# The order of the token products between the feature blocks of a mixer kernel

## The chip, the cores and the metric

The kernel runs on one core of a Trainium2 chip. The metric is the device time of one execution in microseconds (us). A core has five engines that run side by side, each working through its own instructions in their order: TensorE (PE, with its weight loads PEld), VectorE (DVE), ScalarE (ACT), GpSimd (POOL) and SyncE (SP). The last two mostly issue DMAs here.

## The reference

`x` has 8 batches of 4096 tokens with 192 features. A windowed weighted sum over the last seven tokens ("attention") comes first, with weights from a softmax; then a token mixer and a channel mixer, each with a ReLU between two matrix products:

```python
w = exp(weight_gen - max); w = w / (sum(w) + 1e-9)        # over 7 taps, 8 heads
x = einsum('bshk,bskhg->bshg', w, x_unfolded)             # each token with the six before it
h = maximum(x^T @ w_tok1, 0) @ w_tok2                     # over the tokens of a batch: 4096 -> 256 -> 4096
u = x + h^T
out = u + maximum(u @ w_ch1, 0) @ w_ch2                   # over the features: 192 -> 1536 -> 192
```

The four weight matrices come in as float64; the kernel converts them itself. Products are float32, or three float32r products of high and low parts.

## The kernel before, in words

Tokens are handled in 64 blocks (chunks) of 512, eight to a batch (`NCH = 8`, `NG = 64`). Four streams of work are laid into each other.

*Channel products.* Block `g` has six slots (`p` = 0 to 5, `NP = 6`). In each, `channel1(g, p)` multiplies u by 256 of the 1536 hidden columns (ten matmuls into the PSUM tile `ph`, line 496), ScalarE takes the ReLU (line 499) and VectorE the low part (line 500), and `channel2` multiplies the `h` of two slots before by the second weights (lines 514 and 516) into `acc`. It runs two slots behind, so slots 0 and 1 of block `g` still hold products of block `g - 1`; in slot 1 `store(g - 1)` adds `acc` to u (line 528) and writes the result out.

*Token products.* `token1(m)`, the first phase, multiplies chunk `m` of the attention's result by the first token weights and adds to `h1s` (lines 397, 398, 406 and 408; 415 in float32); after the eighth chunk of a batch the sum becomes `h1`. `token2_half(m, half)`, the second phase, multiplies `h1` by the second token weights of chunk `m`, in two halves (lines 449 and 450; 447 in float32), and VectorE adds the attention's result to give u (lines 456 and 458). So the second phase of a batch needs the first phase of all its chunks. Batches 0 and 1 do this in float32, the others in three float32r products; batch 2 makes the split weights and keeps them in DRAM.

*The pieces of u.* After the second half, `columns_of(m)` turns u from rows to columns: a transpose of 32x32 squares on VectorE (line 468), 24 copies on ScalarE in twelve items of two (line 476), then `split_u`: `a_hi` and the high part of `uc` on ScalarE (lines 424 and 425), `a_lo` and the low part of `uc` on VectorE (lines 426 and 429). `channel1(m, 0)` needs all of them.

*Attention.* VectorE makes chunk `m` in 13 operations (lines 200 and 208) and for every second chunk a softmax. A ring of nine buffers holds the results, so attention for chunk `m` waits until the second phase of chunk `m - 9` is done. `two_parts` then splits the chunk for the first phase (lines 222 and 225).

`ph`, the first phase's `th` and the second phase's `up` take turns in two PSUM buffers. `acc`, the token weights' tiles `w1` and `w2` and the tile `xh` have one buffer each.

The order is written by a planner in Python while the kernel is built. `at` holds its estimate of when TensorE, ScalarE and VectorE will be free, `on` adds an operation with its cost, and `pump(limit)` takes pieces from `chains` (the pieces of u, the attention, weight loads and splits) until VectorE is filled to `limit`. Column copies ("u", planned at 200 ns each) are taken only if they can start within 400 ns of the later of ScalarE and TensorE. What is issued decides the order on every engine; when it runs is settled on the chip by semaphores. At the end of each slot of block `g` there is room for one token product, and lines 820 to 830 choose it: the first phase of the next chunk, if it is ready and in slot 1 (`LAG - 1`) or less than eight chunks ahead of `g` (one more in the last block of a batch); else the next half of the second phase of chunk `g + 1`, if begun; else its first half, if `w2` and `h1` are in and the PSUM buffer is free by the plan. What is left after six slots is done at the end of the block.

Of the kernel before, what the change touches and what calls it, by code (L numbers as in the profile page):

```python
# [21 lines left out]
def mixer_kernel(ctx: ExitStack, tc: tile.TileContext, x, wg, wt1, wt2, wc1, wc2, out):  # L22
# [10 lines left out]
    NCH = S // N  # L33
# [5 lines left out]
    NG = B * NCH  # L39
    RING = NCH + 1  # L40
    F1, F2 = 2, 2
    LAG = 2
# [214 lines left out]
    w1t, w2t, rawt = {}, {}, {}  # L257
# [92 lines left out]
    def convert_channel(which, n, pool=None):  # L350
        out = []
        yield from convert(rawt.pop((which, n)), NF2 * D if which == "c2" else HF, out)
        yield "n", 0, lambda: raw_free()
        v, = out
        if which == "w1a":
            cs = slice(n * HF, (n + 1) * HF)
            yield from split(w1a_hi[:, cs], w1a_lo[:, cs], v)
        elif which == "c2":
            fs = slice(n * NF2, (n + 1) * NF2)
            yield from split(w2s[:, fs, 0:D], w2s[:, fs, D:2 * D], v.rearrange("p (f d) -> p f d", f=NF2))  # L360
        else:
            two = pool.tile([P, KA, CT, D], F32, tag="pr", name="prk", bufs=3)
            two = two.rearrange("p k t d -> p (k t d)").bitcast(F32R)
            hi, lo = two[:, 0:HF], two[:, HF:2 * HF]
            yield from split(hi, lo, v)
            for src, dst in ((hi, w1c_hi), (lo, w1c_lo)):
                for j in range(2):
                    for at in (0, DC):
                        yield "a", 730, lambda src=src, dst=dst, j=j, at=at: nc.scalar.copy(
                            dst[at:at + DC, j * HF:(j + 1) * HF], src[j * DC:(j + 1) * DC, :].bitcast(F32))  # L370

        def last():
            state["vals"] -= 1
            done.add((which, n))
        yield "n", 0, last

    h1s, h1t = {}, {}
# [10 lines left out]
    def token1(m):  # L388
        b, i = divmod(m, NCH)
        w = w1t.pop(m)  # L390
        th = ps_w.tile([P, 2, 512], F32, tag="w", name="th")
        if b >= F1:
            xh = xht.pop(m)
            for r in range(KR):
                for c in range(CT):
                    rs = slice(r * P, (r + 1) * P)
                    nc.tensor.matmul(th[:, r, 0:2 * D], w[:, c, 0, rs], xh[:, c, :], start=c == 0, stop=False)  # L397
                    nc.tensor.matmul(th[:, r, 0:D], w[:, c, 1, rs], xh[:, c, 0:D], start=False, stop=c == CT - 1)  # L398
        else:
            token1_float(th, w, m, 0, CT - 1)  # L400
        yield
        if i == 0:
            h1s[b] = late.tile([P, KR, D], F32, tag="h1s", name="h1s")
            nc.scalar.copy(h1s[b], th[:, :, 0:D])
        else:
            nc.vector.tensor_add(h1s[b], th[:, :, 0:D], h1s[b])
        if b >= F1:
            nc.vector.tensor_add(h1s[b], th[:, :, D:2 * D], h1s[b])
        if i == NCH - 1:
            make_h1(b, h1s.pop(b))  # L410
# [124 lines left out]
    at = {"pe": 0.0, "act": 0.0, "dve": 0.0}  # L535
# [5 lines left out]
    SLACK0 = 1000  # L541
    SLACK_M = 400
    LATE = 300
    FIRST = 0
    C1, C2 = 2290, 2264
    TOP, LOW = 1040, 1135
    h_at, w_at, h1_at = {}, deque([0.0, 0.0]), {0: 0.0}
    free = {"acc": 0.0, "u": 0.0}
    ready = deque()

    def on(engine, cost, *after):
        at[engine] = max(at[engine], *after, 0.0) + cost
        return at[engine] + HOP

    class Chain:
# [4 lines left out]
        def next(self):  # L560
            self.item = next(self.items, None)
# [19 lines left out]
    def add_chain(items, wait=None):  # L581

        chains.append(Chain(items, max(at["pe"], at["dve"]) + LOAD if wait is None else wait))

    def pump(limit):

        scalar = not state["rush"] and any(c.item is not None and c.item[0] == "u" for c in chains)
        while True:
            best = None
            for c in chains[1:] + chains[:1]:  # L590
                if c.blocked() or c.item is None:
                    continue
                kind = c.item[0]
                if kind == "u":

                    start = max(at["act"], c.wait)
                    end = max(at["pe"], w_at[0]) + C1 + LATE
                    if state["late"] or start <= max(at["act"], at["pe"]) + 400 and start + c.item[1] <= end:
                        best = c
                        break  # L600
                    continue
                if kind in "as" and c.wait > max(at["act"], at["pe"]):
                    continue
                if kind == "s":
                    if scalar == 0:
                        scalar = 1
                        best = c
                        break
                    continue
                if kind in "an":  # L610
                    best = c
                    break
                start = max(at["dve"], c.wait)
                if best is None or start + 100 < max(at["dve"], best.wait):
                    best = c
            chains[1:] = [c for c in chains[1:] if c.item is not None or c.blocked()]
            if best is None:
                return
            if best.item[0] == "v" and max(at["dve"], best.wait) + best.item[1] > limit:
                return  # L620
            best.issue()
# [54 lines left out]
    with tc.tile_pool(name="pro", bufs=1) as pro:  # L676
# [9 lines left out]
        def start(items):  # L686

            items = iter(items)
            for _ in range(4):
                next(items)[2]()  # L690
            return items
# [48 lines left out]
        last = start(convert_channel("w1a", 1))  # L740
# [21 lines left out]
    def do_token1():  # L762
        m, t = ready.popleft()
        it = token1(m)
        next(it)
        end = on("pe", 2264 if m >= F1 * NCH else 2600, t, w_at.popleft())
        state["token1"] = m
        pump(end + SLACK_M)
        next(it, None)
        w_at.append(on("dve", 1000 if m >= F1 * NCH else 500, end))  # L770
        if m % NCH == NCH - 1:
            h1_at[m // NCH] = on("act", 420, w_at[-1])
            if m >= F2 * NCH:
                h1_at[m // NCH] = on("dve", 480, h1_at[m // NCH])
        if m + 1 < NG:
            add_chain(load_w1(m + 1))
# [17 lines left out]
    def token1_ready():  # L794
        return ready and ready[0][0] in w1t and ready[0][1] <= at["pe"] + 100

    for g in range(NG + 1):
        parts = None if g + 1 < NG else iter(())
        state["rush"] = g == 0
        for p in range(NP if g < NG else LAG):  # L800
            if g == 0:
                need(lambda: (2 * p + 2) * P <= HF or ("w1a", 1) in done)
            if g == 0 and p >= LAG:
                need(lambda: ("c2", 2 * (p - LAG) // NF2) in done)
            if g < NG:
                channel1(g, p)
                end = on("pe", C1, w_at.popleft(), free["u"] if p == 0 else 0.0)
                end = on("act", TOP, end)
                h_at[g, p] = on("dve", LOW, end)
                w_at.append(h_at[g, p])  # L810
            n = g * NP + p - LAG
            if n >= 0:
                prev = divmod(n, NP)
                channel2(*prev)
                on("pe", C2, h_at.pop(prev), free["acc"] if prev[1] == 0 else 0.0)
            if p == LAG - 1 and g > 0:
                store(g - 1)
                free["acc"] = on("dve", 2000, at["pe"] + HOP) - 570
            pump(next_lo() + (SLACK if g > NCH else SLACK0))
            if token1_ready() and (p == LAG - 1 or ready[0][0] < g + NCH + ((g + 1) % NCH == 0)):  # L820
                do_token1()
            elif parts is not None:
                next(parts, None)
            elif p >= FIRST and g + 1 in w2t and (g + 1) // NCH in h1t \
                    and max(w_at[0], h1_at[(g + 1) // NCH]) <= at["pe"]:
                parts = do_token2(g + 1)
                next(parts)
            else:
                continue
            pump(next_lo() + SLACK)  # L830
        if parts is None:
            need(lambda: g + 1 in w2t)
            while (g + 1) // NCH not in h1t:
                need(token1_ready)
                do_token1()
            parts = do_token2(g + 1)
        for _ in parts:
            pass
        if g + 1 < NG:
            need(lambda: g + 1 in ut)  # L840
# [29 lines left out]
```

## Time and profile before

| | |
|---|---|
| three runs, median | 2344.61 us (2344.28 to 2345.2) |
| the profiled execution, its own time | 2343.91 us |
| its span in the profile | 2342.1 us |
| busy: TensorE, VectorE, ScalarE | 2196.7, 1842.1, 1085.0 us |
| matmuls | 12256 |
| mean granted TensorE clock | 0.978 |

The times of the page and of the time lines count from the span's start; a line such as L496 is that line of the kernel. A row of a group gives its line, engine, operation, output and inputs, shape, count, busy time and the mean in ns, then the idle time before it. A row of waits names who waited for whom, the sum in us, how often, and the longest. A matmul's busy time overlaps with the next one's, so the time between starts tells more than the durations. Block 0 begins after the prologue, at 129.7 us; the last block has a tail in which only `store` is left.

### The profile page before, as it was taken

Reading aid. Unit: us, or ns where it says so; the run is one execution under the profiler, and the core shown is the slowest. Engines: PE = TensorE matmul, PEld = TensorE weight load, DVE = VectorE, ACT = ScalarE, POOL = GpSimd, SP = SyncE. Lnnn points to the kernel's source line nnn. Section 1 sums busy time; section 2 is a strip of 40 time slices with the busy share of each in tenths; the row PEclk is TensorE's granted clock in tenths of the full one; section 3 lists DMA queues with packets and bytes.
Section 4 is the critical chain, followed back from the end, with each engine's and each line's share of the span. In section 5 each row is a group of like instructions: output and inputs, shape, how many; then the busy total and the mean of one; then the engine's idle time right before and its main releaser. Section 6 shows DMA issues by size and latency. Waiting matters only on the chain.

```text
span 2342.1 us, 30675 instructions
## 1 busy us (share of the span) xinstructions
PE 2196.7 (94%) x12256; PEld 1962.0 (84%) x12256; DVE 1842.1 (79%) x2231; ACT 1085.0 (46%) x2265; POOL 58.4 (2%) x104
## 2 busy tenths in 40 slices
PE   7869989999998999999999999999999999999998
PEld 5558878888887888888888888888888888899997
DVE  8889887878876888879887888869887798844443
ACT  4675443544534355345434434444443454344443
POOL 0000000000000000000000000000000000000000
PEclk9989999999999999999999999999999999999999
DMA  7733131223241333313332232332233132211110
GB/s 282 233 133 140 63 106 70 100 97 114 92 156 62 108 113 135 120 64 124 123 107 99 105 122 80 116 112 104 101 107 120 63 124 103 73 55 46 46 42 21
DMA packets 52127, 244.69 MB, mean 104 GB/s; under 512 B 6008, under 2 KB 15736, under 8 KB 38672
## 3 DMA queue, kind: packets, MB, share of 16 engines
q1 hardware_dynamic: 43360, 196.58, 24.3%
q0 software_dynamic: 8624, 46.14, 4.9%
q8 instruction: 97, 1.59, 0.3%
q14 instruction: 46, 0.38, 0.0%
HBM read 192.36 MB, written 50.33 MB: 104 GB/s over the span
## 4 chain that ended last, share of the span: by engine, by line
PE 38%; ACT 19%; DVE 14%; issue 11%; DMA 1%; POOL 0%; POOLq 0%; ACTq 0%; SPq 0%; DVEq 0%
PE ph L496 17%; ACT a_f L476 9%; PE acc L514 9%; ACT c_f L476 4%; PE acc L516 4%; ACT h L499 4%; DVE h L500 3%; DVE xa L208 3%; PE th L397 3%; DVE pr L200 3%; PE up L449 2%; DVE uc L429 1%; PE th L398 1%; DVE a_lo L426 1%; DMA w<-s 1%
## 5 line engine op out<-in xcount | busy, mean ns | idle before, releaser
L514 PE MATMUL acc<-w2s,h 128*128 128x384 f32 x3072 | 902.1, 358 | 0.0
L499 ACT ACTIVATE h<-ph 128x1024 fp32r<-128x1024 f32 x384 | 392.8, 1023 | 1004.4 <-PE ph L496 980.3
L516 PE MATMUL acc<-w2s,h 128*128 128x192 f32 x3072 | 773.5, 252 | 0.0
L500 DVE SCALAR_TENSOR_TENSOR h<-ph,h 128x1024 fp32r<-128x1024 f32 x384 | 468.3, 1220 | 294.3 <-ACT h L499 292.7
L516 PEld LDWEIGHTS acc<-w2s,h 128*128 128x128 f32 x3072 | 591.3, 192 | 16.0
L514 PEld LDWEIGHTS acc<-w2s,h 128*128 128x128 f32 x3072 | 583.3, 190 | 16.0
L496 PE MATMUL ph<-a_hi,w1a_hi 128*128 128x512 f32 x768 | 321.6, 419 | 58.9 <-ACT a_hi L424 33.9
L496 PE MATMUL ph<-uc,w1c_hi 128*128 128x512 f32 x768 | 311.7, 406 | 44.2 <-DVE uc L429 44.2
L200 DVE TENSOR_TENSOR pr<-xt,wn 128x768 f32<-128x768 f32 x336 | 318.2, 952 | 4.1
L208 DVE TENSOR_TENSOR xa<-xa,pr 128x768 f32<-128x768 f32 x336 | 319.7, 952 | 1.0
L496 PE MATMUL ph<-a_lo,w1a_hi 128*128 128x512 f32 x768 | 306.8, 399 | 6.0 <-DVE a_lo L426 6.0
L476 ACT COPY a_f<-t 32x128 f32<-32x128 f32 x1024 | 302.6, 295 | 16.6 <-DVE t L468 5.5
L496 PE MATMUL ph<-a_hi,w1a_lo 128*128 128x512 f32 x768 | 305.6, 398 | 0.0
L496 PE MATMUL ph<-uc,w1c_lo 128*128 128x512 f32 x768 | 305.2, 397 | 0.0
L496 PEld LDWEIGHTS ph<-uc,w1c_hi 128*128 128x128 f32 x768 | 146.6, 191 | 97.6 <-DVE uc L429 49.4
L496 PEld LDWEIGHTS ph<-a_hi,w1a_hi 128*128 128x128 f32 x768 | 146.5, 191 | 87.4 <-ACT a_hi L424 37.3
L496 PEld LDWEIGHTS ph<-a_lo,w1a_hi 128*128 128x128 f32 x768 | 146.6, 191 | 45.8 <-DVE a_lo L426 14.4
L496 PEld LDWEIGHTS ph<-uc,w1c_lo 128*128 128x128 f32 x768 | 147.4, 192 | 30.1
L496 PEld LDWEIGHTS ph<-a_hi,w1a_lo 128*128 128x128 f32 x768 | 148.0, 193 | 16.0
L476 ACT COPY c_f<-t 32x128 f32<-32x128 f32 x512 | 152.0, 297 | 7.4
L528 DVE TENSOR_TENSOR ur<-acc,ur 128x384 f32<-128x384 f32 x256 | 136.2, 553 | 8.3 <-PE acc L516 3.9
L449 PE MATMUL up<-h,w 128*128 128x384 f32 x384 | 116.4, 359 | 0.0
(70 smaller groups left out, 1914.8 us busy)
## 6 DMA issues: line engine op xcount, KB each, us to landing
w<-s SPq DMA_DIRECT2D x80, 1024.0 KB
xt<-in_x_dram SPq DMA_DIRECT2D x56, 960.0 KB
out_dram<-ur POOLq DMA_DIRECT2D x63, 384.0 KB, 4.9
raw<-in_moe_w_tok_dram SPq DMA_DIRECT2D x16, 1024.0 KB
s<-w POOLq DMA_DIRECT2D x16, 1024.0 KB, 4.1
val<-s SPq DMA_DIRECT2D x24, 512.0 KB
wg<-in_weight_gen_dram SPq DMA_DIRECT2D x64, 112.0 KB
s<-val SPq DMA_DIRECT2D x8, 512.0 KB
```

Source lines behind the costliest of these rows:

```text
L200: nc.vector.tensor_mul(dst.rearrange("p t (h g) -> p (t h) g", h=H).rearrange("p (o n) g -> p o n g", o=1), x_k, w)
L208: nc.vector.tensor_add(box["acc"], box["acc"], box.pop(k))
L397: nc.tensor.matmul(th[:, r, 0:2 * D], w[:, c, 0, rs], xh[:, c, :], start=c == 0, stop=False)
L398: nc.tensor.matmul(th[:, r, 0:D], w[:, c, 1, rs], xh[:, c, 0:D], start=False, stop=c == CT - 1)
L449: nc.tensor.matmul(up[:, j, 0:2 * D], w[:, k, 0, cs], h1[:, k, :], start=k == 0, stop=False)
L476: nc.scalar.copy(dst[to:to + Q, :].rearrange("p (c n j) -> p c n j", c=CT, n=NQ)[:, :, n, :], box["t"][n * Q:(n + 1) * Q, :, d, :])
L496: nc.tensor.matmul(ph[:, j, :], w[:, fs], u, start=n == 0, stop=n == len(steps) - 1)
L499: nc.scalar.activation(h[:, :, 0, :], ph, AF.Relu)
L500: nc.vector.scalar_tensor_tensor(h[:, :, 1, :], ph, 0.0, h[:, :, 0, :].bitcast(F32), op0=ALU.max, op1=ALU.subtract)
L514: nc.tensor.matmul(ps[:, 0:2 * D], h[:, j, 0, cs], w2s[:, f, :], start=f == 0, stop=False, **kw)
L516: nc.tensor.matmul(ps[:, 0:D], h[:, j, 1, cs], w2s[:, f, 0:D], start=False, stop=f == NF - 1, **kw)
L528: nc.vector.tensor_add(u[:, t, :], a[:, :, l * D:(l + 1) * D], u[:, t, :])
```

## The change: both halves of the second phase in consecutive slots, then the first phase

Only the choice of the token product at the end of a slot changes. `halves` marks that the second half is still to come. The first phase goes first only in the last block of a batch as long as the batch that follows has no `h1`. Otherwise a begun second phase is finished in the next slot; the first half of chunk `g + 1` is taken as soon as it is possible, with 300 ns of tolerance in the test; and then the first phase of chunks up to `g + 8`, in any slot. The constant `FIRST` was 0 and goes.

```diff
+        halves = []
...
-            if token1_ready() and (p == LAG - 1 or ready[0][0] < g + NCH + ((g + 1) % NCH == 0)):
+            last = (g + 1) % NCH == 0 and (g + 1) // NCH not in h1t and g + 1 < NG
+            if token1_ready() and last:
                 do_token1()
-            elif parts is not None:
+            elif parts is not None and len(halves) > 0:
+                halves.pop()
                 next(parts, None)
-            elif p >= FIRST and g + 1 in w2t and (g + 1) // NCH in h1t \
-                    and max(w_at[0], h1_at[(g + 1) // NCH]) <= at["pe"]:
+            elif parts is None and g + 1 in w2t and (g + 1) // NCH in h1t \
+                    and max(w_at[0], h1_at[(g + 1) // NCH]) <= at["pe"] + 300:
                 parts = do_token2(g + 1)
                 next(parts)
+                halves.append(1)
+            elif token1_ready() and ready[0][0] <= g + NCH:
+                do_token1()
             else:
                 continue
             pump(next_lo() + SLACK)
```

More of the change, by code (lines that the diff above doesn't have):

```diff
@@ L543, in mixer_kernel @@
     LATE = 300
-    FIRST = 0
     C1, C2 = 2290, 2264
```

## The prediction

> **What bounds the kernel now.** I read the totals first, then TensorE's waits, then busy time by stretches, then the time lines of VectorE and ScalarE around the waits.
>
> ```profile
> PE 2196.7 (94%) x12256; PEld 1962.0 (84%) x12256; DVE 1842.1 (79%) x2231; ACT 1085.0 (46%) x2265; POOL 58.4 (2%) x104
> ```
> ```profile
> PE ph L496 <- DVE uc L429: 44.2, 54, 2.3
> PE ph L496 <- ACT a_hi L424: 33.9, 12, 9.7
> PE ph L496 <- DVE h L500: 24.6, 28, 7.0
> ...
> PE ph L496 <- DVE a_lo L426: 6.0, 3, 3.2
> ```
>
> TensorE bounds it, and nearly all its idle time lies ahead of ph, the first channel product. For 84.1 us (44.2 + 33.9 + 6.0) it waits for the split pieces of u (a_hi, a_lo, uc) at the start of a block, and for 24.6 us until VectorE has emptied the PSUM buffer that the next ph takes. What this costs is seen block by block: in the next rows the columns are stretch, length, then busy us of PE, PEld, DVE, ACT and POOL, the granted clock and the DMA. The bounds are starts of blocks: 1 to 7, 8 to 14, 15 to 22, 31 to 38, then the pair 31 and 32, the six 33 to 38, then single blocks 28, 29, 33 and 57, and three short stretches behind waits.
>
> ```profile
> 167.40:425.80 258.40, 241.71 (x1335) 217.06 (x1334) 220.47 (x264) 130.19 (x252) 9.49 (x15) 0.97 0.28 99
> 425.80:674.40 248.60, 234.57 (x1319) 212.23 (x1317) 204.22 (x249) 113.78 (x244) 9.12 (x16) 0.98 0.27 100
> 674.40:968.30 293.90, 270.50 (x1505) 242.18 (x1506) 238.08 (x297) 130.56 (x279) 9.13 (x16) 0.96 0.32 115
> 1241.30:1514.40 273.10, 262.04 (x1507) 237.13 (x1506) 229.02 (x289) 122.48 (x271) 5.36 (x9) 0.99 0.30 106
> 1241.30:1313.20 71.90, 67.45 (x378) 60.70 (x377) 50.51 (x65) 30.78 (x70) 1.08 (x2) 0.95 0.28 101
> 1313.20:1514.40 201.20, 194.59 (x1131) 176.43 (x1130) 178.50 (x225) 91.70 (x202) 4.29 (x7) 1.00 0.31 108
> 1141.00:1174.50 33.50, 32.49 (x191) 29.46 (x190) 30.40 (x40) 15.46 (x35) 1.59 (x2) 1.00 0.31 104
> 1174.50:1207.90 33.40, 32.40 (x190) 29.34 (x189) 27.07 (x34) 14.87 (x34) 0.54 (x1) 1.00 0.32 112
> 1313.20:1347.30 34.10, 32.51 (x190) 29.43 (x189) 32.05 (x40) 14.76 (x33) 0.54 (x1) 1.00 0.30 109
> 2122.10:2151.60 29.50, 29.50 (x174) 27.11 (x173) 13.82 (x18) 14.08 (x32) 0.54 (x1) 1.00 0.14 50
> 1279.90:1285.40 5.50, 4.81 (x11) 3.29 (x12) 2.25 (x3) 0.49 (x1) 0.00 (x0) 0.50 0.00 0
> 498.80:502.40 3.60, 3.60 (x18) 3.60 (x17) 2.98 (x4) 1.02 (x1) 0.00 (x0) 0.62 0.53 156
> 533.00:536.60 3.60, 3.16 (x18) 2.89 (x19) 3.29 (x5) 1.03 (x1) 0.00 (x0) 1.00 0.00 0
> ```
>
> Block 57 has no first-phase product and no attention, and TensorE never stops: 29.5 us. One first-phase product takes 2.27 us (1152.78 to 1155.05 below), so a block without waits takes 31.8. Block 29 takes 33.4: 1.6 lost. The pair 31 and 32, where a batch ends, takes 71.9 against 63.6: 8.3 lost. The time line of TensorE in block 28 shows where, and behind it stand three waits of other blocks.
>
> ```profile
> 1146.09 0.36 PE L449 MATMUL up<-h,w 128*128 128x384 f32 x1
> ...
> 1148.13 0.50 PE L496 MATMUL ph<-a_hi,w1a_hi 128*128 128x512 f32 x1 [0.74 <-DVE h L500]
> ...
> 1152.78 0.36 PE L397 MATMUL th<-xh,w 128*128 128x384 f32 x1
> ...
> 1155.05 0.41 PE L496 MATMUL ph<-a_hi,w1a_hi 128*128 128x512 f32 x1
> ...
> 1160.77 0.42 PE L496 MATMUL ph<-a_hi,w1a_hi 128*128 128x512 f32 x1
> ...
> 1175.57 0.51 PE L496 MATMUL ph<-uc,w1c_hi 128*128 128x512 f32 x1 [0.27 <-DVE uc L429]
> ```
> ```profile
> 496.77 0.47 PE L496 MATMUL ph<-uc,w1c_hi 128*128 128x512 f32 x1 [2.29 <-DVE uc L429]
> ...
> 533.44 0.47 PE L496 MATMUL ph<-uc,w1c_hi 128*128 128x512 f32 x1 [2.29 <-DVE uc L429]
> ...
> 1279.92 0.80 PE L496 MATMUL ph<-a_hi,w1a_hi 128*128 128x512 f32 x1 [3.15 <-ACT a_hi L424]
> ```
>
> Slot 0 holds a half of the second phase (1146.09), slot 1 the first phase, slot 2 the other half, which ends at 1160.77. At batch ends two first-phase products come ahead, so the halves sit in slots 2 and 3 and the wait grows to 3.15 us. A long wait also costs clock: behind it the clock was 0.50 for 5.5 us.
>
> **The change part by part.** No operation is added or removed. *The second half moves from slot 2 to slot 1*, past one slot and one first-phase product. From 1155.05 to 1160.77 is one slot with a half, 5.72 us; less that half's own 1.13 (it has half the matmuls of a first-phase product) that is 4.6 for the slot, and 2.27 for the product gives 6.9 us earlier. What follows it is the chain that makes u's pieces: the transpose, 24 column copies, the casts, the two subtractions. In block 28:
>
> ```profile
> 1162.16 0.98 DVE L468 STREAM_TRANSPOSE t<-ur 128x768 f32<-128x768 f32 x1
> ...
> 1174.83 0.69 DVE L429 TENSOR_TENSOR uc<-c_f,uc 64x512 fp32r<-64x512 f32 x1
> ```
> ```profile
> 1164.25 4.90 ACT L476 COPY a_f<-t 32x128 f32<-32x128 f32 x16
> ...
> 1169.69 1.01 ACT L499 ACTIVATE h<-ph 128x1024 fp32r<-128x1024 f32 x1
> 1170.72 1.84 ACT L476 COPY c_f<-t 32x128 f32<-32x128 f32 x6
> ```
>
> It ran from 1160.77 to 1175.52, 14.8 us, and uc is wanted 0.7 us after the block's start (1175.57 less the 0.27 waited). It is late by tenths; 6.9 us earlier it has over 6 to spare. Then the 0.74 wait for h in slot 0 is next: VectorE empties ph late there because u was late and because products of the attention stand ahead of it. Attention for a chunk is let in by the second half nine chunks before, so it too starts a slot and a product earlier, and fewer of its operations reach the next slot 0. I keep 0.4 us per block (between none, as in block 57, and 0.9, the 0.74 with its delay): half of the blocks have a softmax in the same slots. The copies have a cost of their own: a copy takes 0.31 us (4.90 for 16), the planner counts 0.2, so 24 of them may stand 2.5 us longer than planned ahead of the ReLU of slot 3, as 18 did ahead of the one at 1169.69. I count nothing: the buffer that this ReLU and VectorE empty is wanted again in slot 5, two slots (9.1 us) after its own ph began, of which ph takes 2.3, ReLU and VectorE's pass 2.3. Past 4.5 us of lateness TensorE would stop there by the excess. *The first phase moves from slot 1 to slot 2.* Its cast of the next xh and its two adds go with it. The cast waits on ScalarE for the product's end, now behind copies; its chunk is wanted a block later, over 25 us of cover. *DMAs:* w2's reload now stands ahead of w1's in SP's queue; each has one buffer and is wanted again over 20 us later (w2 after four slots and a product, w1 after a block). The chain of waits has one such load at the batch's end:
>
> ```profile
> 1248.91 4.78 DMA w<-s
> ```
>
> It takes 4.8 us, so both stay hidden, and the back-to-back first-phase products that waited for it disappear. POOL's stores follow the same operations in the same order. *At batch ends* the one product that is needed comes first, then the halves in slots 1 and 2, one slot earlier than now. I keep 1.6 us for the next block's start, as in block 29 (whose halves ended in slot 2), 0.4, and 0.5 for the new hidden cost there: the sums and ReLU of the first phase now have one slot of 4.55 us (between 0 and 1.3). That leaves 2.5 of 8.3. *The 0.3 us of tolerance* in the test for the first half lets it into slot 0 more often; cost nothing, since the slot would hold it anyhow.
>
> **Sum.** Against 31.8 a block. Blocks 33 to 38: 201.2 - 190.8 = 10.4, left 2.4, saved 8.0; pair: 8.3 - 2.5 = 5.8. Four groups of eight like this (23 to 54): 4 x 13.8 = 55. Blocks 15 to 22: 293.9 - 254.6 = 39; split of the second weights rides on VectorE there, I leave 12: 27. Blocks 8 to 14: 248.6 - 222.7 = 26; waits of 2.29 and the clock behind them go, float32 products stay, leaving 7: 19. Blocks 1 to 7: 36; VectorE is busy 220.5 of what would be 223, so it soon bounds: 22 left, 14 saved. Together 115. The profiled execution took 2343.9 (median 2344.6): **2229 us**. Bounds: the 0.4 between 0 and 0.9 for some 44 blocks, 15 to 22 left with 5 to 25, the rest by 8: 2200 to 2262.
>
> **The rivals.**
>
> *A: as forecast, 69%.* For it: block 57 has the new order and its pieces are done 4.4 us ahead of the block's end at 2151.6.
>
> ```profile
> 2146.52 0.69 DVE L429 TENSOR_TENSOR uc<-c_f,uc 64x512 fp32r<-64x512 f32 x1
> ```
>
> *B: VectorE takes half of it back, 20%.* Block 33 is against A: in block 32 the halves sat in slots 0 and 1, with attention, yet block 33 took 34.1.
>
> ```profile
> 1294.05 2.20 DVE L528 TENSOR_TENSOR ur<-acc,ur 128x384 f32<-128x384 f32 x4
> ...
> 1299.74 0.97 DVE L468 STREAM_TRANSPOSE t<-ur 128x768 f32<-128x768 f32 x1
> ```
> ```profile
> 1302.14 1.02 ACT L499 ACTIVATE h<-ph 128x1024 fp32r<-128x1024 f32 x1 [2.87 <-PE ph L496]
> 1303.06 4.89 ACT L476 COPY a_f<-t 32x128 f32<-32x128 f32 x16
> ```
>
> The store and an attention add stood ahead of the transpose, and the copies stood behind the ReLU of slot 3, though the transpose ended at 1300.7. Block 32 had no first-phase product in slot 2; the issue of copies behind such a product, which the new order has, is what lets them in before. Where VectorE still lags, 0.8 us stays in steady blocks, 5 in the pairs, and half in 1 to 22: 4 x (5.6 + 3.3) + 28 gives 64 saved, 2280.
>
> *C: a pile-up in slot 1, slower, 6%.* There VectorE now has h, the four stores (2.20) and two adds (with their wait 1.4, from 1160.77 to 1162.16), and ph and the accumulators of slot 2 wait for them. The stores of block 32 ended at 1296.25, 1.1 us before they were wanted (from their start on, a half of 1.13 and a ph of 2.3 were still to come). Beyond a lag of 1.1 us TensorE stops. A softmax adds 3.3 us of VectorE in every second block (30.40 in block 28 against 27.07 in 29).
>
> ```profile
> L200 DVE TENSOR_TENSOR pr<-xt,wn 128x768 f32<-128x768 f32 x336 | 318.2, 952 | 4.1
> ```
> ```profile
> 1151.79 1.23 DVE L500 SCALAR_TENSOR_TENSOR h<-ph,h 128x1024 fp32r<-128x1024 f32 x1 [0.60 <-ACT h L499]
> ```
>
> If the softmax and one such product (0.95) stood ahead of h there, 3.15 us would be lost, the very wait of block 32, and behind it 5.5 us at half clock (2.75): 5.9 in 27 blocks is 159, and 2388. It decides from 115 / 27 = 4.3 us lost in each on. Against it: VectorE stood idle for 0.60 before h in slot 1 of block 28, softmax and all. [...]
>
> *D: the halves stay where they are, 5%,* because w2 or the buffer isn't ready in the planner's slot 0: 2344. Against it: blocks from 8 on begin their first half there already.
>
> **How the numbers follow.** About 0.2% (4.7 us) can be told from no change. A and B are faster, and a little of D: 0.89; D and edges: 0.04; C: 0.07. 2195 to 2300 leaves out C, D and thin edges of A and B, under 2 in 10.
>
> **What would show it.** Right: TensorE's waits for uc and a_hi fall from 78 to under 25 us; steady blocks near 32.2, the pair near 66, clock above 0.95 there; copies start in slot 2. Wrong: waits for h (24.6 now) grow past 40 (B), waits in slot 2 for h or the accumulators (C), or first halves still ahead of a first-phase product (D).

## The result, and the profile after

The changed kernel takes 2270.76 us (median of four runs, 2268.67 to 2271.11) against 2344.45 us for the kernel before: a ratio of 0.9685, 95% interval 0.9669 to 0.9702, some 74 us faster. The forecast was 2229 us with a range of 2195 to 2300, so the direction and the range held, but only two thirds of the 115 us came. One execution of all that follow, of the kernel with the copies at 300 ns, ran at a mean granted clock of 0.654 (0.991 in the others) and took 2949.67 us; the ratio given there is of the other three.

The waits of TensorE in the changed kernel (who waited for whom, sum in us, times, longest):

```profile
PE ph L496 <- DVE h L500: 49.7, 37, 6.6
...
PE ph L496 <- DVE h1s L408: 9.9, 6, 3.0
PE ph L496 <- ACT a_hi L424: 9.7, 1, 9.7
PE ph L496 <- DVE uc L429: 3.3, 7, 1.1
```

Before, the three pieces of u cost 84.1 us of waiting; now 13.0, of which one wait of 9.7 is block 0's and was there before. But the wait for h, the emptying of the PSUM buffer, has doubled from 24.6 to 49.7 us, and there is a new one, for `h1s`.

Busy time by stretches of the changed kernel, in the columns of the prediction: blocks 1 to 7, 8 to 14, 15 to 22, the pair 31 and 32, the six 33 to 38, and the single blocks 28 (with a softmax) and 29 (without).

```profile
169.00:414.50 245.50, 235.37 (x1333) 214.40 (x1333) 223.41 (x267) 130.03 (x252) 9.51 (x15) 0.99 0.31 108
414.50:651.30 236.80, 229.65 (x1318) 209.46 (x1317) 204.13 (x251) 114.77 (x245) 8.59 (x15) 0.99 0.30 107
651.30:923.30 272.00, 260.29 (x1505) 236.84 (x1505) 236.78 (x296) 129.41 (x277) 9.66 (x17) 0.99 0.34 124
1190.00:1257.20 67.20, 65.18 (x378) 58.99 (x377) 55.81 (x71) 31.23 (x69) 1.08 (x2) 1.00 0.30 107
1257.20:1457.30 200.10, 194.42 (x1130) 177.89 (x1129) 173.76 (x219) 91.36 (x201) 4.29 (x7) 0.99 0.31 109
1091.00:1124.40 33.40, 32.15 (x189) 29.47 (x189) 30.30 (x40) 15.52 (x34) 1.59 (x2) 1.00 0.32 105
1124.40:1156.60 32.20, 32.09 (x189) 29.41 (x189) 27.09 (x34) 14.94 (x33) 0.54 (x1) 1.00 0.33 116
```

The pair fell from 71.9 to 67.2 us and its clock rose from 0.95 to 1.00: the 3.15 us wait and the slow products behind it are gone. The six blocks hardly moved, from 201.2 to 200.1. A block without softmax now takes 32.2, close to the 31.8 without waits; one with softmax still takes 33.4. What it loses is lost in one place, in slot 0, behind the first half (1095.5 to 1096.7):

```profile
1097.93 0.50 PE L496 MATMUL ph<-a_hi,w1a_hi 128*128 128x512 f32 x1 [1.25 <-DVE h L500]
```

The cause lies a block earlier. ScalarE and then VectorE of the changed kernel from slot 2 on (block 28; the same shape stands in block 27):

```profile
1107.19 4.90 ACT L476 COPY a_f<-t 32x128 f32<-32x128 f32 x16
1112.12 2.46 ACT L476 COPY c_f<-t 32x128 f32<-32x128 f32 x8
1114.61 0.62 ACT L424 CAST a_hi<-a_f 128x512 fp32r<-128x512 f32 x1
...
1115.65 0.83 ACT L222 CAST xh<-xa 128x768 fp32r<-128x768 f32 x1
1116.39 1.02 ACT L499 ACTIVATE h<-ph 128x1024 fp32r<-128x1024 f32 x1
```
```profile
1115.26 0.69 DVE L426 TENSOR_TENSOR a_lo<-a_f,a_hi 128x512 fp32r<-128x512 f32 x1 [1.57 <-ACT a_hi L424]
1116.51 0.96 DVE L225 TENSOR_TENSOR xh<-xa,xh 128x768 fp32r<-128x768 f32 x1 [0.56 <-ACT xh L222]
...
1118.20 1.23 DVE L500 SCALAR_TENSOR_TENSOR h<-ph,h 128x1024 fp32r<-128x1024 f32 x1
```

All 24 copies, both casts of u and the cast of xh stand in one piece ahead of slot 3's ReLU. The planner's price decides this: besides the test on a copy's start, it takes a copy only if, at that price, it ends no later than 0.3 us after the end of the next channel product (lines 596 and 597 of the changed kernel). At 24 times 200 ns all of them pass; they take 7.4 us. VectorE, whose next operations need their results, stands idle for 1.57 and 0.56 us, then works without a gap, and is still behind when slot 0 of the next block comes. In slot 0 of block 28, behind the same row of copies in block 27, h starts at 1096.66, two microseconds after the end of its ReLU (1093.34 and 1.03 long).

```profile
1093.34 1.03 ACT L499 ACTIVATE h<-ph 128x1024 fp32r<-128x1024 f32 x1 [3.53 <-PE ph L496]
...
1096.66 1.22 DVE L500 SCALAR_TENSOR_TENSOR h<-ph,h 128x1024 fp32r<-128x1024 f32 x1
```

Over the whole kernel these two waits of VectorE come to 98 us:

```profile
DVE a_lo L426 <- ACT a_hi L424: 66.1, 48, 3.3
...
DVE xh L225 <- ACT xh L222: 31.9, 39, 2.0
```

The other new wait is in slot 4 of the first block of a batch (block 32). The first chunk's first-phase product is not added but copied out of PSUM, by ScalarE (line 404), and that copy stands behind 14 column copies:

```profile
1241.67 4.30 ACT L476 COPY a_f<-t 32x128 f32<-32x128 f32 x14 [3.10 <-DVE t L468]
...
1246.72 0.47 ACT L404 COPY h1s<-th 128x384 f32<-128x384 f32 x1
...
1247.22 0.56 DVE L408 TENSOR_TENSOR h1s<-th,h1s 128x384 f32<-128x384 f32 x1 [3.88 <-ACT h1s L404]
```
```profile
1247.83 0.50 PE L496 MATMUL ph<-a_hi,w1a_hi 128*128 128x512 f32 x1 [1.08 <-DVE h1s L408]
```

The theory from here on, L: what is left is VectorE's lag, made in slot 3 by copies that the planner takes for shorter than they are. Rival F: VectorE is simply full in the blocks with a softmax (30.3 us busy). Rival V: the planner's prices of VectorE's own operations are too low.

### The profile page after: what moved, and what is told of

The parts are those of the page before. It is cut to its first block, busy times and chain, and to the rows that moved or that the text cites. A ratio compares the mean times of both kernels' runs of the same rounds, so it can differ in the third digit from the quotient of the medians.

```text
span 2269.1 us, 30604 instructions
## 1 busy us (share of the span) xinstructions
PE 2161.0 (95%) x12256; PEld 1948.0 (86%) x12256; DVE 1843.1 (81%) x2231; ACT 1085.4 (48%) x2265; POOL 58.4 (3%) x104
## 3 DMA queue, kind: packets, MB, share of 16 engines
q8 instruction: 97, 1.59, 0.3%
## 4 chain that ended last, share of the span: by engine, by line
DVE 31%; issue 31%; ACT 19%; PE 17%; DMA 1%; POOL 1%; POOLq 0%; SPq 0%; ACTq 0%; DVEq 0%
PE ph L496 10%; ACT a_f L476 8%; DVE h L500 8%; DVE xa L208 6%; DVE pr L200 5%; ACT c_f L476 4%; PE acc L514 3%; ACT h L499 3%; PE acc L516 2%; DVE prk L240 1%; DVE ur L528 1%; DVE uc L429 1%; ACT xh L222 1%; DVE xh L225 1%; PE up L449 1%
## 5 line engine op out<-in xcount | busy, mean ns | idle before, releaser
L496 PE MATMUL ph<-a_hi,w1a_hi 128*128 128x512 f32 x768 | 319.3, 416 | 71.1 <-DVE h L500 49.7
L476 ACT COPY a_f<-t 32x128 f32<-32x128 f32 x1024 | 302.6, 296 | 43.4 <-DVE t L468 32.1
L496 PE MATMUL ph<-uc,w1c_hi 128*128 128x512 f32 x768 | 303.0, 395 | 3.3 <-DVE uc L429 3.3
L496 PEld LDWEIGHTS ph<-uc,w1c_lo 128*128 128x128 f32 x768 | 145.5, 189 | 31.9
```

Of the source, the lines that this page charges most:

```text
L476: nc.scalar.copy(dst[to:to + Q, :].rearrange("p (c n j) -> p c n j", c=CT, n=NQ)[:, :, n, :], box["t"][n * Q:(n + 1) * Q, :, d, :])
L496: nc.tensor.matmul(ph[:, j, :], w[:, fs], u, start=n == 0, stop=n == len(steps) - 1)
```

## The experiments

**Which part of the change gave what.** One kernel has the new choice only in the last block of each batch, another in all other blocks:

```diff
+            new = (g + 1) % NCH == 0        # the other kernel: != 0
+            if not new and <the old choice> ...
+            elif new and <the new choice> ...
```

> The new choice only in the last block of each batch, the old one in all others. If the parts add up: the pairs around a batch's end give 4 x 4.7 (71.9 to 67.2 us), the pair 15 and 16 some 9 and 7 and 8 none, so about 28 of the 74 us: 2316. If the clock gate made most of it, the pairs alone give 40 and more: under 2305.

Measured: 2300.87 us, ratio 0.9817 (0.9802 to 0.9831): 43 us of the 74, so the last blocks alone give more than the 28 expected, and the time is that of the second case. The pair 31 and 32 and the six behind it in that kernel:

```profile
1218.30:1284.10 65.80, 64.53 (x378) 58.73 (x377) 57.25 (x73) 31.18 (x70) 1.08 (x2) 1.00 0.31 110
1284.10:1484.70 200.60, 194.61 (x1130) 176.35 (x1129) 172.37 (x217) 90.95 (x202) 4.29 (x7) 1.00 0.31 108
```

The pair is better than in the full change (65.8 against 67.2), the six about the same (200.6, 200.1). That the clock made most of the 43 us is not shown: of the 6.1 us that the pair gained (71.9 to 65.8), 2.9 are TensorE's busy time (67.45 to 64.53 for the same 378 matmuls, at a clock of 0.95 and then 1.00), which I take for the cost of the lower clock, and 3.2 are waits. The four pairs like it give some 24 us; most of the rest came from blocks 15 to 22 (293.9 to 276.8).

> The new choice in all blocks but the last of each batch, where the old one stays. If the parts add up: the rest of the 74 us, about 46: 2299. The last block keeps its halves in slots 2 and 3, so TensorE still waits some 3 us for a_hi at six starts of a batch. If the parts depend on each other (the old last block starts the next chunk's first phase, so the blocks behind it have none in slot 2) less is left: above 2310.

Measured: 2303.7 us, 0.9828 (0.9813 to 0.9843), 40 us, between its two cases. The parts give 83 us one by one and 74 together, so some 9 us are lost between them. Of the 40 us, 36 come from blocks 1 to 22, and only 5 from blocks 23 to 54 (1092.3 to 1086.9): there the wait for u became a wait for h. In the changed kernel, too, a steady block with a softmax takes the 33.4 us of before, one without went from 33.4 to 32.3, and what these gained the first two blocks of a batch gave back (block 32: 33.3 to 35.0, block 33: 34.1 to 35.4). The 300 ns of tolerance play no part: without them the planner writes the same instructions in the same order on every engine.

**The true price of a copy.**

```diff
-            yield "u", 200 * len(part), lambda part=part: move(part)
+            yield "u", 300 * len(part), lambda part=part: move(part)
```

> The changed kernel with one number of the planner changed: a column copy is planned at 300 ns and not at 200 (measured 306). Theory L (lag): what is left in slot 0 (TensorE waits 49.7 us for h) comes from slot 3, where too many copies stand ahead of the ReLU and VectorE stands idle for 1.6 us before a_lo and 0.6 before the low part of xh (98 us in all). With true prices fewer copies go there: those two waits fall under 50 us, the wait for h under 35, time 2245 to 2262. Rival F (full): VectorE simply has 30.3 us of work in the blocks with a softmax; the waits move about but the time stays at 2265 to 2276.

Measured: 2217.92 us, ratio 0.9461 (0.9445 to 0.9477), better than the theory's range. The profile is that of a second run of the same kernel:

> The same kernel as with the copies planned at 300 ns, for a profile at an undisturbed clock. Theory L: 2216 to 2219 again; TensorE's waits for h at 15 us or less (49.7 in the changed kernel), VectorE's for a_hi and the cast of xh under 50 (98).

Measured: 2216.94 us, 0.9456 (0.9439 to 0.9473). TensorE's waits, then VectorE's two, then slot 3 on ScalarE (block 28), then h in slot 0 of block 28 on VectorE, then busy time of block 28 and of the six blocks 33 to 38:

```profile
PE ph L496 <- ACT a_hi L424: 10.5, 2, 9.7
PE ph L496 <- DVE h L500: 9.6, 4, 7.0
PE ph L496 <- DVE uc L429: 8.9, 12, 1.1
```
```profile
DVE xh L225 <- ACT xh L222: 17.1, 8, 3.1
...
DVE a_lo L426 <- ACT a_hi L424: 3.2, 4, 1.6
```
```profile
1080.01 0.84 ACT L222 CAST xh<-xa 128x768 fp32r<-128x768 f32 x1
1080.75 1.02 ACT L499 ACTIVATE h<-ph 128x1024 fp32r<-128x1024 f32 x1
1081.79 1.22 ACT L476 COPY c_f<-t 32x128 f32<-32x128 f32 x4
```
```profile
1062.56 1.23 DVE L500 SCALAR_TENSOR_TENSOR h<-ph,h 128x1024 fp32r<-128x1024 f32 x1
```
```profile
1058.90:1090.80 31.90, 31.90 (x190) 29.47 (x190) 30.11 (x40) 15.59 (x34) 1.10 (x2) 1.00 0.32 110
1222.80:1414.90 192.10, 191.63 (x1129) 176.58 (x1128) 174.74 (x221) 91.90 (x201) 4.29 (x7) 1.00 0.32 113
```

Four copies and the casts of u go behind the ReLU, VectorE's two waits fall from 98 us to 20, and block 28, with the same softmax and 30.1 us of VectorE, takes 31.9 us with TensorE busy in all of it. The same two sums of the attention and two operations of the softmax stand ahead of h in slot 0 as in the changed kernel, but h now starts at 1062.56, right behind its ReLU (1061.50 and 1.03 long): so it was not their place that made h late. Rival F falls: VectorE at 94% of a block is not too full.

**The same order, shorter copies.** A price changes the order; this kernel changes only the length. Each copy moves half of its columns, so the kernel leaves out half of u's columns and multiplies zeros in their place; every operation of ScalarE and VectorE stands in the order of the changed kernel:

```diff
-  nc.scalar.copy(dst[...][:, :, n, :], box["t"][n * Q:(n + 1) * Q, :, d, :])
+  nc.scalar.copy(dst[...][:, 0:2, n, :], box["t"][n * Q:(n + 1) * Q, 0:2, d, :])
```

> The changed kernel, same order on every engine, with each column copy moving 64 of its 128 columns (the other half of u's columns stays at zero, so half of the tokens are computed from zeros); two memsets ahead of block 0 are the only operations added. From 295 ns at 128 columns and 620 at 512 a copy should take some 240 ns: 1.3 us less per block ahead of slot 3's ReLU. Theory L: VectorE's waits for a_hi and the cast of xh (98 us) fall to 30 to 60, TensorE's for h (49.7) to under 35, time 2235 to 2258. If the order and not the copies' length makes the lag: 2264 to 2274.

Measured: 2216.14 us, 0.9455 (0.9441 to 0.9469). A copy took 242 ns:

```profile
DVE xh L225 <- ACT xh L222: 33.0, 40, 3.1
...
DVE a_lo L426 <- ACT a_hi L424: 19.7, 41, 2.0
PE ph L502 <- DVE h L506: 18.0, 12, 5.6
```

The waits fell as theory L has it (98 to 53, and 49.7 to 18.0), and the time by more than its range: 24 copies shorter by 54 ns are 1.3 us a block, and some 52 of the 55 us came from blocks 1 to 54. From block 26 on a steady block with a softmax gained these 1.3 us in full (33.4 to 32.1), one without the 0.4 that it still lost (32.3 to 31.9). With the order the same, it is the length of the copies ahead of the ReLU that made the lag.

**VectorE's own prices.**

```diff
-        cost = 70 + NE * 1.05        # attention: 876 ns
+        cost = 150 + NE * 1.05       # 956 ns; a_lo from 540 to 700
```

> The changed kernel with VectorE's prices put up to what was measured: attention operations from 876 to 956 ns, a_lo from 540 to 700; copies stay at 200. Theory L: the stall comes from the copies; a little less attention ahead of h: 2258 to 2272. Rival V: VectorE's own low prices make the lag: under 2245.

Measured: 2272.62 us, 0.9695 (0.968 to 0.971), no different from the changed kernel and a hair above theory L's range. Rival V falls, as far as these two prices go.

**More and less than the true price.**

> The changed kernel with the copies planned at 250 ns, between 200 (2270.8 us) and 300 (2217). Theory L: each copy is still 56 ns too long in the plan, half of the error: part of the stall stays in slot 3, 2228 to 2250. If it is enough that the last copies go behind the ReLU: 2212 to 2220.

Measured: 2227.72 us, 0.9508 (0.9492 to 0.9524): at the lower edge of theory L's range, for four fifths of the gain of 300 come with half of the price's error.

> The changed kernel with the copies planned at 400 ns, more than the 306 that they take. Theory L: between 300 and 400 there is nothing more to win in slot 3, and the pieces of u have over 3 us to spare: 2215 to 2228. If the gain goes on with the price (the delay of the copies itself helps, not the true price): under 2212. If the pieces of u come late again: above 2235, with waits for uc and a_hi.

Measured: 2272.89 us, 0.9694 (0.9678 to 0.9709): neither of the first two, but the third, that u's pieces come late again.

```profile
PE ph L496 <- ACT a_hi L424: 29.0, 13, 9.7
PE ph L496 <- DVE a_lo L426: 15.2, 18, 2.3
...
PE ph L496 <- DVE uc L429: 11.6, 22, 1.6
```

I had reckoned with 3 us to spare in all blocks. The ordinary ones from block 25 on have them, and run at 31.9 there too; the blocks of the third batch, where the weight split rides along (283 us in blocks 15 to 22, against 261 at 300 ns), the ends and starts of the batches (71 us for the pair 31 and 32, against 68) and the short blocks from 57 on (30.6, against 29.6) have not.

**The price without the new order.** The kernel before, with 300 for 200.

> The kernel before, old order, with the copies planned at 300 ns. If the price of the copies gives the gain by itself (the order doesn't matter): under 2260. If the two need each other: in the old order the pieces of u are late for want of time, which no price gives; some copies go a slot later and the pieces come later still, while the h of slot 4 comes sooner: 2325 to 2365.

Measured: 2392.05 us, 1.0205 (1.0189 to 1.0221): slower than expected in the second case. TensorE's waits in that kernel:

```profile
PE ph L496 <- DVE uc L429: 56.6, 56, 1.1
...
PE ph L496 <- ACT a_hi L424: 47.4, 24, 9.7
...
PE ph L496 <- DVE a_lo L426: 25.3, 45, 3.2
PE ph L496 <- DVE h L500: 7.7, 2, 6.8
```

The late h is gone here too (24.6 to 7.7), and u's pieces cost 129 instead of 84 us. In the old order the low price was the better one: in block 28 six of the copies stood behind slot 3's ReLU with it, and twelve with the true price, where there was no time for them. It is the new order that has the time, and with it the true price is worth 54 us.

**The new wait at a batch's start.**

```diff
-            nc.scalar.copy(h1s[b], th[:, :, 0:D])
+            nc.vector.tensor_copy(h1s[b], th[:, :, 0:D])
```

> The changed kernel with one operation on another engine: the copy of the first chunk's first-phase product out of PSUM (one per batch) goes from ScalarE to VectorE. Theory: in the block after a batch's end this copy stands behind 14 to 17 column copies on ScalarE, and slot 4 waits for its buffer (9.9 us in six waits, with the clock behind two of them 14.7 us). On VectorE the six waits vanish: about 2256. Rival: VectorE lags there anyway, the add would have been late too: 2266 to 2274.

Measured: 2266.69 us, 0.9674 (0.9657 to 0.969), in the rival's range. TensorE's waits for `h1s` are gone from the profile, but those for h grew:

```profile
PE ph L496 <- DVE h L500: 55.1, 40, 6.3
```

Blocks 25, 33 and 41, each the second of its batch, lose some 4 us where they had lost 2.0, 3.6 and 2.0. VectorE, no longer held up for 3.88 us by that copy, waits 1.59 us a little later for the cast of xh, behind the same 14 column copies. TensorE's wait for h after slot 0 of these blocks grew from 1.7 to 2.2 or 2.3 us, and behind it the clock was 0.76 to 0.79 for 7 us in all three, where in the changed kernel it had fallen in block 33 alone (0.72 over 6 us; 1.00 in blocks 25 and 41). Removing a wait ahead of a lagging engine moved it on, and part of the gain went back through the clock.

**A version that beats both.** Price 300, but 200 for the first chunk of a batch, whose second half comes a slot later:

```diff
+            yield "u", (200 if m % NCH == 0 else 300) * len(part), lambda part=part: move(part)
```

> The changed kernel with the copies planned at 300 ns, but at 200 for the first chunk of a batch (which has its second half one slot later). At 300 all starts of a batch wait: u's pieces come after slot 5's ReLU (4.2, 4.2, 2.7 and 2.7 us lost in blocks 24, 32, 40 and 48). Theory: at 200 they come before it, 1 to 2 us are lost there, and six starts give 8 to 14 us: 2203 to 2209. If the late h in slot 0 of those blocks takes it back: 2212 to 2218.

Measured: 2205.75 us, ratio 0.941 (0.9396 to 0.9424), within the theory's range: 138 us less than the kernel before and 65 less than the changed one. Pair 31 and 32, and the six behind it:

```profile
1147.00:1212.80 65.80, 64.80 (x377) 58.84 (x377) 53.39 (x69) 31.27 (x69) 1.08 (x2) 1.00 0.31 110
1212.80:1405.00 192.20, 191.78 (x1131) 176.76 (x1130) 174.83 (x221) 91.92 (x201) 4.29 (x7) 1.00 0.32 113
```

The six are at 32.0 a block. Some 2 us stay in the pair.

## Why the prediction was right or wrong

- *The second half earlier, u's pieces in time: right.* The waits for uc and a_hi went from 78 to 13.0 us; "under 25" was asked for. No block from 25 to 55 but the first of a batch waits for u.
- *The wait for h then goes to 0.4 us a block: wrong, and this is the step that failed.* It became 1.25 in blocks with a softmax; without one there is none in the list, and TensorE is idle for 0.11 in all. With what hangs on it the six blocks lose 9.3 us (200.1 - 190.8), not 2.4. The prediction saw that 24 copies would stand 2.5 us longer than planned ahead of slot 3's ReLU, and wrote "I count nothing", because the buffer behind that ReLU has two slots. That cover is real for TensorE: in block 28 that ReLU came over 3 us late, and slot 5 did not wait. But VectorE waits behind the same copies, for a_hi and the cast of xh, and h comes later in its own order; its lag is what reached slot 0. The shorter copies and the true price show it.
- *Batch ends: the mechanism right, the size near.* 3.6 us (67.2 - 63.6) stay in the pair, not 2.5. The start of block 32 loses some 1.5 us, about what was kept for it. Wrong was that "its two adds go with it": for the first chunk of a batch one of the two is a copy on ScalarE, which the column copies hold up, a new wait (9.9 us in six) that the prediction did not have. The hidden cost that it did have there, 0.5 us for the first phase's sums and ReLU, did not show as a wait of TensorE.
- *The groups.* Blocks 1 to 7 saved 12.9 us (258.4 - 245.5; 14 forecast), 8 to 14 saved 11.8 (19), 15 to 22 saved 21.9 (27), and the four groups of eight from 23 on about 28 (55). Nearly two thirds of the miss is in the last. The near hit in blocks 1 to 7 was luck: 22 us were left there because VectorE "soon bounds", but with the copies at 300 ns the same blocks take 229.8 us, with VectorE busy for 220.4 of them. What was left was mostly the lag.
- *The time: in the range by its width.* The bounds of the sum itself, 2200 to 2262, were missed by 9 us (its three terms added up in full would have given 2196 to 2272). The stated range held because it took in rival B as well.
- *Rivals.* B's time (2280; with 30 for half of the 60 us, and not 28, its sum gives 2278) was nearer than A's, and a steady block kept about what B said, 1.0 us on the mean of blocks 28 and 29 for 0.8. Its reason was not what happened: it had the copies behind the ReLU of slot 3, as in block 32 of the kernel before; the first-phase product in slot 2 did let them in ahead, as A has it, and there were too many of them. C did not come: TensorE's waits name no accumulators. D: from block 1 on all halves sit where the change puts them.
- *What was to show it.* Steady blocks near 32.2: only those without a softmax. The pair near 66: 67.2, clock 1.00. Waits for h past 40 were the sign of B, and came at 49.7.

## What to carry to other kernels

When work is moved earlier, ask of every engine that waits behind it, not only of the one that bounds: a stall that TensorE's buffers cover may still put VectorE behind, and the lag comes out in the next place with little cover. A planner's wrong price can be right for the order in which it was found: here the price of 300 ns for a copy was 54 us better than 200 after the order had changed, and 48 us worse before. So after a change of order, measure the prices again, one at a time.

## What the runs showed of the hardware

In the kernel before, one of the two waits of 2.29 us was followed by a granted clock of 0.62 over 3.6 us (from 498.8 us on), the other by 1.00 (from 533.0 on). Shorter waits, too, were followed by a lower clock in some places and not in others. With the copies at 300, blocks 32 and 40 start with the same two waits, but over the 6 us from the block's start on the first had a clock of 0.75 and the second of 1.00. The waits and these 6 us in that kernel:

```profile
1188.03 0.50 PE L496 MATMUL ph<-a_lo,w1a_hi 128*128 128x512 f32 x1 [0.49 <-DVE a_lo L426]
...
1189.61 0.68 PE L496 MATMUL ph<-uc,w1c_hi 128*128 128x512 f32 x1 [1.08 <-DVE uc L429]
```
```profile
1448.43 0.50 PE L496 MATMUL ph<-a_lo,w1a_hi 128*128 128x512 f32 x1 [0.48 <-DVE a_lo L426]
...
1450.02 0.50 PE L496 MATMUL ph<-uc,w1c_hi 128*128 128x512 f32 x1 [1.08 <-DVE uc L429]
```
```profile
1186.80:1192.80 6.00, 4.43 (x13) 3.00 (x12) 4.55 (x6) 0.48 (x1) 0.00 (x0) 0.75 0.21 67
1447.20:1453.20 6.00, 4.44 (x23) 3.36 (x22) 4.76 (x7) 1.51 (x2) 0.00 (x0) 1.00 0.20 70
```

So two waits of 1.6 us together within 2.1 us were followed by a lower clock in one block and not in the other. In the changed kernel the same holds of single waits: behind the wait of 1.70 us after slot 0 of block 33 (until 1264.60) the clock was 0.72 over 6 us, behind the 1.69 us of block 25 (until 998.85) it stayed at 1.00. Why equal waits end differently no run here shows.
